# Windowed attention followed by a sine-gated MLP on one core: attention output written straight into the full x, first loads reordered, mask setup cut, and the global-token inserts moved from the MLP part to the attention part

## The chip, the cores and the metric

The kernel runs on one core of one Trainium2 chip. The metric is the time of one execution on the device in microseconds (us), as the median of several executions. Each kernel was also run once under the hardware profiler, and all readings of a profile below are from that execution. Its length is called the span; it is 2.2 us below the median for the kernel before.

Five engines work in parallel, and the text uses the profile's names for them: PE (matmuls; PEld is its weight load), DVE (vector engine), ACT (scalar engine, activation functions), POOL (GpSimd), and SP, which here only issues DMAs. DMAs are also issued by POOL and by ACT, and an issue takes time on the engine's queue.

## The reference, cut to what matters

```python
# q, k, v: (8 batches, 8 heads, 576 tokens, 64); 8 global token indices
def _attn_ref(q, k, v, global_idx):
    scores = (1 / sqrt(64)) * q @ k^T
    mask = |i - j| <= 32, or i is global, or j is global
    attn = softmax(where(mask, scores, -1e9))
    return attn @ v

def _moe_ref(x, w_in, w_out, alpha):       # x: (4608, 512); d_ff = 2048
    h = x @ w_in
    s = np.sin(alpha * h)
    g = h + s * s / (alpha + 1e-09)
    return g @ w_out
```

x is the attention output, with the heads side by side. All matmuls of the kernels run in bf16.

## The kernel before

The kernel walks through nine iterations p. Iteration p does attention of batch p (for p below 8) and then the first matmul of the MLP for chunk p of 512 tokens. The second matmul of chunk p-1 fills PE's gaps during attention of batch p. A batch has 576 tokens and a chunk 512, so eight batches give nine chunks, and the last iteration has no attention.

Attention is cut into 8 units: 4 head pairs (hp) times 2 halves (hf) of the tokens. A unit is scores `Sp` (PE), `E = exp` (ACT), `E * MASK` (DVE), the denominator `den` (PE), its reciprocal as exp(-ln) (ACT), the numerator `num` (PE), and numerator times reciprocal (DVE). These names are in the profile lines below.

The key tile `kTw` of a head pair holds, for each window of 48 queries, 112 window keys and then 8 global keys; `qBD` holds 48 queries and then 8 global queries. The transposes (`stage_T`) bring the batch's own keys and queries, and `globals_in` inserts the global ones, on POOL:

```python
    def globals_in(b, hp):
        nc.gpsimd.tensor_copy(out=kTw[hp][:, :, KB : KB + NG], in_=GT[:, 0, hp, b, ...])
        for t in range(2):
            nc.gpsimd.tensor_copy(out=qBD[hp][pr, :, t, QB:QC], in_=GT[pr, 1, hp, b, ...])
```

Attention writes into a tile of its own batch, `xTb`. At the end the rows of the global tokens are scattered into it by POOL, and DVE copies it to the chunk tiles `xC`, because a chunk spans two batches:

```python
    def stage_G(b, xTb, gn, gd):
        # ... gr = 1 / (gd[0] + gd[1]); gs = gn[0] + gn[1]; xg = gs * gr, on DVE
        for j in range(NG):
            nc.gpsimd.tensor_copy(out=xTb[:, :, bass.ds(pregs[j], 1)], in_=xg[:, :, j : j + 1])
        for c in range(...):                       # the chunks that this batch touches
            nc.vector.tensor_copy(out=xC[c][:, :, ...], in_=xTb[:, :, ...])
```

The first MLP matmul has 16 slots of 128 hidden units. Each slot does 4 matmuls, a sine on ACT, a square on DVE or POOL, and `H2b = S2 * recip + h` on DVE. In slot 10 the next batch's global inserts and the transposes of its first head pair are put in, in slot 13 those of the second:

```python
                eng = nc.vector if nt % 4 == 3 or (c == 0 and nt % 2) else nc.gpsimd
                eng.tensor_tensor(out=S2[:], in0=Sb[:], in1=Sb[:], op=ALU.mult)
    # ...
                def nxt(p=p, psB=psB):
                    shift_v(p + 1)
                    global_v(p + 1)                 # DMA: global values into VW
                    for hp in range(NHP):
                        globals_in(p + 1, hp)
                    stage_T(p + 1, 0, psB, "hb")
                m1.insert(10, nxt)
                m1.insert(13, partial(stage_T, p + 1, 1, psB, "hb"))
```

The prologue loads batch 0, builds the mask and gathers the global tokens' q, k and v. The mask has to know which windows already hold a global token as an ordinary key (`flag`). It gets there through POOL steps that take DVE's results:

```python
    # after the loads, and after about 20 memsets on DVE:
    nc.vector.memset(gcol[:].bitcast(DT.int32), 0)
    nc.scalar.dma_start(out=gcol[KB : KB + NG, :], in_=global_idx[:, None])
    # ...
    nc.vector.tensor_scalar(out=EQ[:], in0=Gf[:], scalar1=Gp[:, 0:1], op0=ALU.is_equal)
    nc.gpsimd.affine_select(out=EQ[:], in_=EQ[:], ...)                   # POOL waits for DVE
    nc.vector.tensor_reduce(out=flag[:], in_=EQ[:], op=ALU.max)          # DVE waits for POOL
    nc.vector.tensor_scalar(out=flag[:], in0=flag[:], ...)
    for base, cm in (...):
        nc.gpsimd.affine_select(out=flag[:], in_=flag[:], ...)           # and again
    # ... DQ = (distance > 32) * flag on DVE
    nc.vector.tensor_tensor(out=MASK[:, :, 0:QB], in0=MB[:], in1=DQ[:], op=ALU.max)
```

The softmax here doesn't subtract the row's maximum and nothing guards it: scores larger than these inputs give would overflow.

## Time and profile before

The time before was 444.24 us (median of three runs, 440.4 to 445.32). The profiled execution took 442.0 us. The page's first part gives busy time per engine, its share of the span, and the number of instructions:

```profile
PE 346.8 (78%) x2396; PEld 183.1 (41%) x2440; DVE 298.1 (67%) x628; ACT 269.3 (61%) x453; POOL 275.1 (62%) x447
```

No engine is full, so averages don't tell what bounds the kernel, and it has to be read stage by stage. Three points in time mark the stages, read from the timeline of PE: the first MLP matmul of an iteration ("MLP start"), the first den matmul of the next attention, and the next MLP start. This table holds them for the kernel before:

| Stage | us |
|---|---|
| start to first den of attention 0 | 36.1 |
| first den of attention 0 to MLP start 0 | 22.4 |
| MLP start 0 to MLP start 1 (period 1) | 53.0 |
| periods 2 to 7 | 44.7, 44.7, 44.6, 46.1, 44.5, 44.4 |
| of a steady period: MLP start to first den / first den to MLP start | 21.8 / 22.8 |
| last MLP start of an attention iteration to the end (tail) | 61.6 |

**The prologue.** The next lines are from the timeline of the kernel before, in order of start: start and duration in us, engine, line, operation, output<-input, count, and in brackets the idle time before it with what ended it.

```profile
16.26 0.32 ACTq L170 DMA_DIRECT2D gcol<-in_global_idx_dram  x1
25.48 0.13 DVE L193 CAST Gp<-gcol 128x1 f32<-128x1 int32 x1
...
28.88 0.18 POOL L201 TENSOR_SCALAR_AFFINE_SELECT EQ<-EQ 128x8 f32<-128x8 f32 x1
29.10 0.16 DVE L206 TENSOR_REDUCE flag<-EQ 128x1 f32<-128x8 f32 x1 [2.59 <-POOL EQ L201]
...
33.87 0.20 POOL L211 TENSOR_SCALAR_AFFINE_SELECT flag<-flag 128x1 f32<-128x1 f32 x1
34.10 0.52 DVE L245 TENSOR_SCALAR DQ<-DQ,flag 128x576 f32<-128x576 f32 x1 [3.36 <-POOL flag L211]
34.66 0.76 DVE L249 TENSOR_TENSOR MASK<-MB,DQ 128x576 bf16<-128x576 f32 x1
...
36.08 0.44 PE L352 MATMUL den<-E,ones_89 128*128 128x336 bf16 x1 [4.39 <-DVE E L342]
```

The scores were exponentiated by 30.92, but the den matmul ran at 36.08, because MASK was written only at 34.66 to 35.42. DVE twice waited for a POOL select of a fifth of a microsecond. On POOL these selects stood behind global inserts and weight-load issues. The index load itself was issued only at 16.26.

**A steady period.** Windows are busy times in a stretch; here the two halves of one steady period of the kernel before, MLP start to first den and first den to MLP start:

```profile
200.84:222.62 21.78, 17.30 (x102) 8.25 (x104) 16.31 (x25) 16.78 (x24) 18.11 (x28) 1.00 0.26 52
222.62:245.44 22.82, 21.24 (x181) 12.29 (x184) 16.32 (x48) 14.90 (x30) 13.32 (x24) 1.00 1.31 112
```

The columns after the length are PE, PEld, DVE, ACT and POOL busy, then the granted PE clock as a share of full speed, the time of the DMA packets as a share of 16 engines (above 1 where packets overlap) and GB/s. In the MLP half POOL is the busiest engine with 18.11 of 21.78 us, while in the attention half it has 9.5 us to spare. From the timeline, the end of POOL's chain and what hangs on it:

```profile
211.36 1.03 POOL L477 TENSOR_TENSOR S_2637<-Sb 128x512 bf16<-128x512 bf16 x1
...
212.34 0.26 POOL L285 COPY kTw_96<-GT 128x96 bf16<-128x96 bf16 x1
...
215.20 0.58 POOL L291 COPY qBD_103<-GT 64x96 bf16<-64x96 bf16 x2
215.87 1.04 POOL L477 TENSOR_TENSOR S_2678<-Sb 128x512 bf16<-128x512 bf16 x1
...
218.86 1.03 POOL L477 TENSOR_TENSOR S_2734<-Sb 128x512 bf16<-128x512 bf16 x1
...
221.41 0.74 DVE L455 SCALAR_TENSOR_TENSOR H2b<-S_2744,recipT,hb 128x512 bf16<-128x512 bf16 x1
222.07 0.91 DVE L342 TENSOR_TENSOR E<-E,MASK 128x672 bf16<-128x672 bf16 x2
...
222.62 0.30 PE L352 MATMUL den<-E,ones_89 128*128 128x336 bf16 x1 [1.87 <-DVE E L342]
```

From 212.34 to 215.78 POOL does inserts in the middle of its squares. Its last square ends at 219.89. DVE's H2b additions follow the squares, its multiplication by the mask follows the additions, and den follows that. The last stretch is DVE's own: once a POOL square has released it at 216.94, it runs without a gap to the mask multiplication, six additions and a square of its own (218.92, 1.25 us).

**The end of attention.** Three lines of the same timeline, from the last scatter to the next MLP start:

```profile
199.54 0.73 POOL L411 COPY xTb<-xg 128x4 bf16 x3
200.30 0.83 DVE L418 COPY xC<-xTb 128x1280 bf16<-128x1280 bf16 x2 [2.14 <-POOL xTb L411]
200.84 9.10 PE L465 MATMUL hb<-xC,w_in 128*128 128x512 bf16 x39 [0.75 <-DVE xC L418]
```

PE waits 0.75 us for the xC copy that follows the scatters.

### The profile page before, as it was taken

Reading aid. Unit: us, or ns where it says so; the run is one execution under the profiler, and the core shown is the slowest. Engines: PE = TensorE matmul, PEld = TensorE weight load, DVE = VectorE, ACT = ScalarE, POOL = GpSimd, SP = SyncE. Lnnn points to the kernel's source line nnn. Section 1 sums busy time; section 2 is a strip of 40 time slices with the busy share of each in tenths; the row PEclk is TensorE's granted clock in tenths of the full one; section 3 lists DMA queues with packets and bytes.
Section 4 is the critical chain, followed back from the end, with each engine's and each line's share of the span. In section 5 each row is a group of like instructions: output and inputs, shape, how many; then the busy total and the mean of one; then the engine's idle time right before and its main releaser. Section 6 shows DMA issues by size and latency. Waiting matters only on the chain.

```text
span 442.0 us, 7238 instructions
## 1 busy us (share of the span) xinstructions
PE 346.8 (78%) x2396; PEld 183.1 (41%) x2440; DVE 298.1 (67%) x628; ACT 269.3 (61%) x453; POOL 275.1 (62%) x447
## 2 busy tenths in 40 slices
PE   1036367599869997899789978998799879989996
PEld 0024223264436443554355445544454345434442
DVE  7556829767587758774878486848784878494520
ACT  0236636574778478756875686658775877564521
POOL 8956359881699269926992699249944910485410
PEclk9999969789999999999999998999999999999999
DMA  9939929996309830993099309940994000100111
GB/s 81 125 67 185 114 18 92 201 170 79 93 5 143 95 90 2 139 104 90 1 134 92 105 2 123 95 114 0 102 116 116 0 25 25 47 1 24 50 47 71
DMA packets 132055, 35.22 MB, mean 80 GB/s; under 512 B 123186, under 2 KB 126002, under 8 KB 132018
## 3 DMA queue, kind: packets, MB, share of 16 engines
q0 software_dynamic: 120896, 19.02, 58.8%
q1 hardware_dynamic: 8034, 15.54, 12.3%
q10 hardware_dynamic: 3088, 0.21, 0.6%
q8 instruction: 19, 0.31, 0.3%
q14 instruction: 18, 0.15, 0.1%
HBM read 38.42 MB, written 9.44 MB: 108 GB/s over the span
## 4 chain that ended last, share of the span: by engine, by line
POOL 33%; issue 27%; PE 16%; DVE 13%; DMA 5%; ACT 3%; POOLq 2%; ACTq 0%
DVE H2b L455 7%; PE ops L499 6%; PE hb L465 6%; DMA QS<-in_q_dram 4%; POOL QS L105 3%; POOL VW_104 L112 3%; POOL KS L105 3%; POOL VW_105 L112 3%; POOL xTb L411 3%; PE hb L499 2%; ACT L472 1%; POOL QS L100 1%; ACT Sb L472 1%; POOL KS L100 1%; POOLq L277 1%
## 5 line engine op out<-in xcount | busy, mean ns | idle before, releaser
L465 PE MATMUL hb<-xC,w_in 128*128 128x512 bf16 x559 | 134.1, 383 | 19.0 <-DVE xC L418 10.0
L472 ACT ACTIVATE Sb<-hb,alphaT 128x512 bf16<-128x512 f32 x144 | 94.5, 687 | 42.8 <-PE hb L465 35.8
L499 PE MATMUL ops<-w_out,H2b 128*128 128x512 bf16 x412 | 105.8, 384 | 2.0 <-ACT osb L506 0.7
L465 PEld LDWEIGHTS <-w_in 128*128 128x128 bf16 x576 | 56.3, 98 | 89.0 <-issue 28.7
L499 PEld LDWEIGHTS <-H2b 128*128 128x128 bf16 x576 | 53.9, 98 | 52.5 <-issue 2.3
L411 POOL COPY xTb<-xg 128x4 bf16 x64 | 12.9, 201 | 85.3 <-DVE xg L409 81.9
L384 DVE TENSOR_TENSOR xTb<-num,rec 64x288 bf16<-64x288 f32 x128 | 57.9, 452 | 7.9 <-PE num L375 6.8
L340 ACT ACTIVATE E<-Sp 128x672 bf16<-128x672 f32 x64 | 46.8, 731 | 14.8 <-PE Sp L333 14.3
L342 DVE TENSOR_TENSOR E<-E,MASK 128x672 bf16<-128x672 bf16 x64 | 31.8, 506 | 19.5 <-ACT E L340 18.5
L359 ACT ACTIVATE lnd<-den 128x288 f32<-128x288 f32 x64 | 26.2, 409 | 23.0 <-PE den L352 23.0
L105 POOL DMA_DIRECT2D QS<-in_q_dram x42 | 32.6, 775 | 6.0 <-DMA w_in<-in_moe_w_in_dram 3.3
L105 POOL DMA_DIRECT2D KS<-in_k_dram x42 | 33.0, 785 | 2.6 <-DMA w_in<-in_moe_w_in_dram 1.8
L506 ACT COPY osb<-ops 128x512 f32<-128x512 f32 x27 | 15.7, 581 | 30.0 <-PE ops L499 29.3
L352 PE MATMUL den<-E,ones_89 128*128 128x336 bf16 x64 | 20.3, 317 | 16.9 <-DVE E L342 16.4
L361 ACT ACTIVATE rec<-lnd 128x288 f32<-128x288 f32 x64 | 28.4, 443 | 2.0
L499 PE MATMUL qp<-w_out,H2b 128*128 128x512 bf16 x105 | 27.7, 379 | 0.4
L299 PE MATMUL Kps<-identb,KS 96*128 96x96 bf16 x192 | 14.7, 217 | 9.3 <-DVE Kps L152 6.4
L112 POOL DMA_DIRECT2D VW_105<-in_v_dram x28 | 21.4, 785 | 0.0
L333 PE MATMUL Sp<-qBD_100,kTw_96 128*128 128x112 bf16 x96 | 8.1, 227 | 16.9 <-DVE H2b L455 10.5
L375 PE MATMUL num<-E,VW_104 128*128 128x112 bf16 x192 | 15.0, 215 | 8.0 <-DVE gn L392 7.2
L112 POOL DMA_DIRECT2D VW_104<-in_v_dram x28 | 21.2, 768 | 0.0
L352 PE MATMUL den<-E,ones_90 128*128 128x336 bf16 x64 | 20.4, 319 | 0.0
(392 smaller groups left out, 605.6 us busy)
## 6 DMA issues: line engine op xcount, KB each, us to landing
out_dram<-osb SPq DMA_DIRECT2D x36, 256.0 KB
KS<-in_k_dram POOLq DMA_DIRECT2D x42, 96.0 KB, 4.0
QS<-in_q_dram POOLq DMA_DIRECT2D x42, 96.0 KB, 4.2
VW_104<-in_v_dram POOLq DMA_DIRECT2D x20, 112.0 KB, 5.1
VW_105<-in_v_dram POOLq DMA_DIRECT2D x20, 112.0 KB, 4.4
w_in<-in_moe_w_in_dram POOLq DMA_DIRECT2D x4, 512.0 KB, 7.9
w_out<-in_moe_w_out_dram POOLq DMA_DIRECT2D x4, 512.0 KB, 11.4
VW_104<-VW_104 SPq DMA_DIRECT2D x4, 384.0 KB
```

The source lines that it names most:

```text
L105: nc.gpsimd.dma_start(out=dst[:, t, :, :], in_=src[b, :, t * TW : (t + 1) * TW, :].rearrange("h p d -> p h d"),)
L112: nc.gpsimd.dma_start(out=W[p0 : p0 + n, par, u, :].rearrange("p (h d) -> p h d", d=D), in_=v[b, :, key0 : key0 + n, :].rearrange("h p d - ...
L340: nc.scalar.activation(out=E[:], in_=Sp[:, :, 0:EW], func=AF.Exp, scale=scale)
L342: nc.vector.tensor_tensor(out=Ev, in0=Ev, in1=MASK[:, hf * NU : (hf + 1) * NU, None, :].to_broadcast([P, NU, 2, QC]), op=ALU.mult,)
L352: nc.tensor.matmul(out=den[:].rearrange("p u c -> p (u c)"), lhsT=on[:], rhs=E[:].rearrange("p a (u t c) -> p (a u) t c", t=2, c=QC)[:, :, ...
L359: nc.scalar.activation(out=lnd[:], in_=den[:, :, 0:QB], func=AF.Ln)
L361: nc.scalar.activation(out=rec[:], in_=lnd[:], func=AF.Exp, scale=-1.0)
L384: nc.vector.tensor_tensor(out=xTb[pr, hp, hf * NU * QB : (hf + 1) * NU * QB].rearrange("p (a u c) -> p a u c", a=2, u=HU), in0=numv[pr, :, ...
L455: nc.vector.scalar_tensor_tensor(out=H2b[:, n_, :], in0=s_[:], scalar=recipT[:, n_ : n_ + 1], in1=h_, op0=ALU.mult, op1=ALU.add,)
L465: nc.tensor.matmul(out=h2[:], lhsT=w_in[:, ci, nt * P : (nt + 1) * P], rhs=xC[c][:, ci, :], start=(ci == 0), stop=(ci == CT - 1),)
L472: nc.scalar.activation(out=Sb[:], in_=h2[:], func=AF.Sin, scale=alphaT[:, nt : nt + 1])
L499: nc.tensor.matmul(out=ops[:], lhsT=H2b[:, nt, ts * P : (ts + 1) * P], rhs=w_out[:, nt, :], start=(nt == 0), stop=(nt == NT - 1),)
```

## The change

Its intent: attention writes its result straight into one tile `xT` of all tokens, which removes the copies to `xC`; the first loads are issued in the order of need; the mask is built from a band of three windows instead of twelve, with no POOL step that takes data from another engine; and the inserts for the next batch go from POOL's full MLP part to the attention part, where POOL has room. Part of the squares move too: in chunks 0 and 1 to ACT and DVE, later from every fourth on DVE to every fifth. Cut to its core:

```diff
+    xT = const.tile([P, CT, NTOK], BF, name="xT")
@@ setup: index loads and the zeroing of VW and Kps first, then the first four K/Q loads
-    nc.vector.tensor_scalar(out=EQ[:], in0=Gf[:], scalar1=Gp[:, 0:1], ...)
-    nc.gpsimd.affine_select(out=EQ[:], in_=EQ[:], ...)
+    # RF, a 0/1 tile made on POOL ahead of time, takes the place of the selects on data
+    nc.vector.scalar_tensor_tensor(
+        out=EQ[:], in0=Gf[:], scalar=Gp[:, 0:1], in1=RF[:, 1:], op0=ALU.is_equal, op1=ALU.mult)
@@
-    for base, cm in ((-KB, 1), (KB + NG - 1, -1)):
-        nc.gpsimd.affine_select(out=flag[:], in_=flag[:], ...)
+    nc.vector.tensor_tensor(out=flag[:], in0=flag[:], in1=RF[:, 0:1], op=ALU.mult)
-    MB = setup.tile([P, NW, QB], F32, name="MB")       # 12 windows
+    MB = setup.tile([P, 3, QB], F32, name="MB")        # first, inner, last window
@@ stage_V writes xT instead of xTb; stage_G:
-                out=xTb[:, :, bass.ds(pregs[j], 1)], in_=xg[:, :, j : j + 1]
-        for c in range(...):
-            nc.vector.tensor_copy(out=xC[c][...], in_=xTb[...])
+                out=xT[:, :, b * S : (b + 1) * S][:, :, bass.ds(pregs[j], 1)], in_=xg[...]
@@ mm1
-                        rhs=xC[c][:, ci, :],
+                        rhs=xT[:, ci, c * CH : (c + 1) * CH],
-                eng = nc.vector if nt % 4 == 3 or (c == 0 and nt % 2) else nc.gpsimd
+                eng = sq(nt)        # nc.scalar: activation(..., func=AF.Square)
+    sq_late = lambda nt: nc.vector if nt % 5 == 4 else nc.gpsimd
+    sq_early = lambda nt: nc.vector if nt % 2 else nc.scalar     # chunks 0 and 1
@@ attention of batch 0
+                    stage_T(0, 0, psA, "qp")
+                    globals_all()                      # cast, transpose, GT
+                    for hp in range(NHP):
+                        globals_in(0, hp, nc.vector)
+                    stage_T(0, 1, psA, "qp")
+                    globals_v_all()                    # VgN cast, recipT
+                    shift_v(0)
+                    global_v(0)                        # DMA VW<-VgN
+                    parts, last = attention(0, psA, {2: 7, 3: 11})   # head pairs 2, 3 at parts 7, 11
+                    with_extra(parts, w_loads, 6, 1)
+                    parts[6] = partial(chain, parts[6], pool_regs)
@@ attention of later batches: the next batch's inserts, on POOL
+                        for hp in range(NHP):
+                            i_ = (10, 12, 14, 16)[hp]
+                            parts[i_] = partial(chain, parts[i_], partial(globals_in, p + 1, hp))
@@ MLP part
-                    for hp in range(NHP):
-                        globals_in(p + 1, hp)
```

A part is one step of attention's unit loop, two for each unit and four ahead of them. Batch 1's loads, and part of batch 2's, move to the MLP part of the iteration before.

## The prediction

> **What bounds the kernel now.** No engine is full: the page has PE 78%, DVE 67%, ACT 61%, POOL 62% of 442.0 us. The timeline shows three stretches.
>
> 1. Prologue, 0 to 58.5 us, when the first MLP matmul starts. The first den matmul runs at 36.08, although the scores were exponentiated by 31. It waits for MASK: the gcol load is issued only at 16.26, behind memsets on DVE; then come POOL selects at 28.88 and 33.87, behind weight-load issues.
> 2. Steady periods, 44.6 us from MLP start to MLP start (e.g. 156.2, 200.84, 245.5). POOL works without pause from 204.01 to 219.88: 12 squares of 1.04 us and 3.3 us of global inserts. DVE's last H2b additions follow it, and attention's first den comes 21.8 us after MLP start (177.96 for the MLP from 156.2). POOL bounds the MLP part.
> 3. The end of attention: last num (195.8), xTb, gr, xg, eight POOL scatters (2.04 us), xC copies (0.83 us), MLP at 200.84. PE works off second matmuls until 200.1, so only 0.7 us is exposed.
>
> **What the change does.**
>
> - Mask: gcol is loaded at once, no POOL step waits for data, the band mask is a quarter in size. By order and durations, DVE finishes MASK near 19 us and the inserts near 22-23; ACT issues loads until 15.5, copies q, reloads its table (1.28). First den near 26 instead of 36. The rest of attention 0 took 22.4 us and loses 1.4 (xC, gr): MLP 0 starts near 47, 11.5 us earlier. Weights should land in time.
> - Batch 1: its loads move to MLP 0 (23 issues of 0.76 = 17.5 us on POOL), so ACT and DVE take the squares there. The inserts and two transposes precede attention 1 (about 4.5 us of latency), but PE does 24 second matmuls there. I expect about 49.5 us instead of 52.9: -3.
> - Period 2: ACT does 8 squares beside sine and copies, about 19.4 us: +1.
> - Periods 3 to 7: POOL has 13 squares instead of 12 plus inserts, and DVE's tail is shorter, as the last square is no longer its own (1.26 us beside POOL; 0.41 alone at 83.66). The Trainium skill, "SBUF — State Buffer", "Who interferes with whom", says that a DVE tensor_tensor with two SBUF inputs contends with GpSimd reads; those durations agree. First den about 18.6 us after MLP start instead of 21.8; 0.7 us from xC. About -3.3 to -3.9 each, -17 for five. The inserts fit between POOL's load issues (end 189.7) and its scatters (198.2).
> - Tail: +0.5 (13th POOL square).
>
> Sum: -11.5 - 3 + 1 - 17 + 0.5 = -30: **414 us, 80% range 402 to 426**. Chances: faster 0.95, same 0.04, slower 0.01.
>
> **What would show it.** First den near 26; first MLP matmul near 47; steady periods of 41 us; POOL's MLP stretch 2 us shorter; inserts in attention without delaying scatters; PE busy nearly unchanged (347 us).
>
> **What would make it wrong.** Weights or late heads arriving after need; PE falling to the halved clock (0.50 from 54 to 62 us after 5.3 us idle; the skill's "TensorE: Matmul & The Clock Gate", Part 1, has this) at attention 1's end, where no second matmuls remain; a second limit in the MLP part (ACT: sines, q copies and table loads are about 15 us) just below POOL; attention being PE-bound, so that an earlier start is lost later; POOL inserts blocking DVE's mask multiplications.

## The result, and the profile after

The changed kernel took 419.47 us (median of four runs, 418.45 to 419.92) against 444.5 us (440.4 to 445.32) of the kernel before, and is correct. The ratio is 0.945, with a 95% interval of 0.939 to 0.951. Here and below a ratio is the mean time of one kernel's fast runs over the mean of the other's fast runs of the same rounds, so it is not quite the ratio of the medians. A run counts as slow when it is over 1.5% above the fastest of its kernel. No run was (the kernel before spreads most, by 1.3%), so all count as fast. The profiled execution took 416.7 us. Busy time by engine:

```profile
PE 347.9 (83%) x2440; PEld 183.4 (44%) x2440; DVE 279.4 (67%) x636; ACT 277.1 (67%) x469; POOL 258.1 (62%) x418
```

PE's work is the same. DVE and POOL lost 19 and 17 us, ACT gained 8. Where the 25.3 us of the span went follows from the same marks as above:

| Stage | before | after | difference | predicted |
|---|---|---|---|---|
| start to first den | 36.1 | 25.5 | -10.6 | -10 |
| first den to MLP start 0 | 22.4 | 27.4 | +5.0 | -1.4 |
| period 1 | 53.0 | 48.9 | -4.1 | -3 |
| period 2 | 44.7 | 45.8 | +1.1 | +1 |
| periods 3 to 7, sum | 224.2 | 207.5 | -16.8 | -17 |
| tail | 61.6 | 61.6 | 0.0 | +0.5 |

One row has the wrong sign: attention 0 became longer. The timeline of PE of the changed kernel shows why:

```profile
25.49 0.72 PE L364 MATMUL den<-E,ones 128*128 128x336 bf16 x2 [1.37 <-DVE E L354]
...
30.64 0.74 PE L387 MATMUL num<-E,VW 128*128 128x112 bf16 x6 [2.97 <-DMA VW<-VgN]
...
33.30 0.68 PE L311 MATMUL Kps<-identb,KS 96*128 96x96 bf16 x6
33.78 0.68 PE L326 MATMUL qp<-identb,QS 96*128 96x96 bf16 x6
35.83 0.72 PE L345 MATMUL Sp<-qBD,kTw 128*128 128x112 bf16 x6 [1.37 <-ACT qBD L333]
```

Before that, the first den was held by something that the prediction doesn't have. The timeline of DVE of the changed kernel:

```profile
24.83 0.25 DVE L284 RECIPROCAL recipT<-alphaT 128x16 f32<-128x16 f32 x1 [1.63 <-DMA alphaT<-in_moe_alpha_dram]
25.00 0.86 DVE L354 TENSOR_TENSOR E<-E,MASK 128x672 bf16<-128x672 bf16 x2
```

E was exponentiated by 23.36, but DVE stood at a reciprocal of `alpha` for 1.63 us, waiting for the load of `alpha`, ahead of the multiplication by the mask. In run 6, whose edit doesn't touch this, the wait was 0.30 us and the first den came at 24.15. No run moved this load on purpose.

The first num waits 2.97 us for the DMA that puts the global values into VW. At 33.30 the head pair 2 is transposed, and the next matmul on PE is that head pair's scores, which wait for the copies of the transposes out of PSUM. The same happens with head pair 3 at 41.69, with a wait of 1.56 us for kTw. The DMA's issue is in the timeline of SP:

```profile
23.22 0.81 SPq L128 DMA_DIRECT2D VW<-VgN  x1
```

The steady period of the changed kernel, in windows from MLP start to first den and from there to MLP start:

```profile
188.79:208.37 19.58, 18.05 (x109) 8.72 (x108) 14.28 (x22) 16.93 (x25) 15.33 (x16) 1.00 0.22 53
208.37:230.38 22.01, 20.43 (x181) 11.98 (x181) 16.24 (x46) 14.66 (x30) 17.34 (x37) 1.00 1.42 120
```

POOL now has 15.33 us of work in the MLP half (18.11 before) and 17.34 us in the attention half (13.32 before), and both halves are shorter. The lines that end the MLP half, from the timeline of POOL, DVE, ACT and PE:

```profile
201.63 3.04 POOL L496 TENSOR_TENSOR S<-Sb 128x512 bf16<-128x512 bf16 x3 [0.28 <-ACT Sb L488]
...
205.18 2.72 DVE L471 SCALAR_TENSOR_TENSOR H2b<-S,recipT,hb 128x512 bf16<-128x512 bf16 x4
205.41 1.28 ACT L442 ACT_TABLE_LOAD   x1
205.47 1.04 POOL L496 TENSOR_TENSOR S<-Sb 128x512 bf16<-128x512 bf16 x1 [0.80 <-ACT Sb L488]
206.70 0.73 ACT L352 ACTIVATE E<-Sp 128x672 bf16<-128x672 f32 x1
207.82 0.50 DVE L354 TENSOR_TENSOR E<-E,MASK 128x672 bf16<-128x672 bf16 x1
208.37 0.45 PE L364 MATMUL den<-E,ones 128*128 128x336 bf16 x2 [0.43 <-DVE E L354]
```

POOL now waits for ACT's sines (0.28 and 0.80 us) instead of the other way round. ACT has E ready at 207.43, DVE finishes its additions at 207.90: two chains end half a microsecond apart. The end of attention has no copy any more; the MLP starts right behind the scatters:

```profile
188.01 0.73 POOL L425 COPY xT<-xg 128x4 bf16 x3
188.79 10.10 PE L481 MATMUL hb<-xT,w_in 128*128 128x512 bf16 x44
```

### The profile page after: what moved, and what is told of

Read it like the earlier page. It is cut to its first block, busy times and chain, and to the rows that moved or that the text cites. A ratio compares the mean times of both kernels' runs of the same rounds, so it can differ in the third digit from the quotient of the medians.

```text
span 416.7 us, 7242 instructions
## 1 busy us (share of the span) xinstructions
PE 347.9 (83%) x2440; PEld 183.4 (44%) x2440; DVE 279.4 (67%) x636; ACT 277.1 (67%) x469; POOL 258.1 (62%) x418
## 4 chain that ended last, share of the span: by engine, by line
PE 42%; ACT 18%; DVE 17%; issue 11%; POOL 10%; POOLq 1%; ACTq 0%
PE hb L481 15%; PE ops L518 13%; ACT Sb L488 7%; DVE H2b L471 6%; PE den L518 5%; DVE xT L397 5%; ACT qBD L333 4%; DVE E L354 3%; POOL S L496 3%; PE num L387 2%; ACT S L494 2%; PE den L364 2%; DVE gn L405 2%; PE hb L518 2%; ACT E L352 2%
## 5 line engine op out<-in xcount | busy, mean ns | idle before, releaser
L481 PE MATMUL hb<-xT,w_in 128*128 128x512 bf16 x576 | 137.5, 387 | 11.0 <-POOL xT L425 8.3
L471 DVE SCALAR_TENSOR_TENSOR H2b<-S,recipT,hb 128x512 bf16<-128x512 bf16 x144 | 101.3, 742 | 48.5 <-POOL S L496 48.5
L488 ACT ACTIVATE Sb<-hb,alphaT 128x512 bf16<-128x512 f32 x144 | 94.1, 685 | 39.6 <-PE hb L481 36.1
L496 POOL TENSOR_TENSOR S<-Sb 128x512 bf16<-128x512 bf16 x91 | 94.4, 1064 | 38.4 <-ACT Sb L488 33.6
L397 DVE TENSOR_TENSOR xT<-num,rec 64x288 bf16<-64x288 f32 x128 | 58.0, 453 | 8.7 <-PE num L387 6.8
L108 POOL DMA_DIRECT2D VW<-in_v_dram x56 | 42.4, 766 | 0.7 <-PE num L387 0.3
L345 PE MATMUL Sp<-qBD,kTw 128*128 128x112 bf16 x384 | 31.1, 220 | 14.0 <-ACT E L352 11.1
L387 PE MATMUL num<-E,VW 128*128 128x112 bf16 x384 | 30.4, 217 | 11.0 <-DVE gn L405 8.1
L333 ACT COPY qBD<-qp 64x576 bf16<-64x576 bf16 x40 | 25.1, 627 | 18.6 <-DMA gN<-in_v_dram 13.7
L525 ACT COPY osb<-ops 128x512 f32<-128x512 f32 x28 | 16.3, 582 | 27.8 <-PE ops L518 27.2
L364 PE MATMUL den<-E,ones 128*128 128x336 bf16 x128 | 30.1, 318 | 5.5 <-DVE E L354 3.9
L345 PEld LDWEIGHTS <-kTw 128*128 128x128 bf16 x384 | 24.5, 102 | 20.9 <-issue 13.9
```

The source lines that it names most:

```text
L108: nc.gpsimd.dma_start(out=W[p0 : p0 + n, par, u, :].rearrange("p (h d) -> p h d", d=D), in_=v[b, :, key0 : key0 + n, :].rearrange("h p d - ...
L333: nc.scalar.copy(out=qBD[hp][pr, :, t, 0:QB], in_=Qps[pr].rearrange("p (i c) -> p i c", c=QB),)
L345: nc.tensor.matmul(out=Sp[:, u // HU, o : o + 2 * QC], lhsT=kTw[hp][:, hf * NU + u, :], rhs=qBD[hp][:, hf * NU + u, :, :], start=True, sto ...
L387: nc.tensor.matmul(out=num[:, u // HU, o : o + 2 * QC], lhsT=W[:, i % 2, i // 2, hp * P : (hp + 1) * P], rhs=E[:, u // HU, o : o + 2 * QC] ...
L397: nc.vector.tensor_tensor(out=xT[pr, hp, x0 : x0 + NU * QB].rearrange("p (a u c) -> p a u c", a=2, u=HU), in0=numv[pr, :, :, t, 0:QB], in1 ...
L471: nc.vector.scalar_tensor_tensor(out=H2b[:, n_, :], in0=s_[:], scalar=recipT[:, n_ : n_ + 1], in1=h_, op0=ALU.mult, op1=ALU.add,)
```

## The experiments

Theories. For the steady periods the theory is the prediction's: POOL's chain of squares and inserts bounded the MLP half, and taking the inserts out of it is the main gain; the rivals are that the new division of squares or the missing xC copies made it. For the prologue the theory is that the mask (index load and POOL selects) was the last thing that attention 0 waited for in the kernel before, and that the changed kernel's loss afterwards comes from the late DMA of global values and from transposes standing directly before their scores. Twelve kernels ran, in four groups, each beside the kernel before on the same chip. "Before" below is the median of that group: 440.93 us (439.87 to 445.02), 442.01 us (439.9 to 444.75) and 444.06 us (439.77 to 445.08), and for run 12 443.76 us (439.99 to 444.9). The kernel before jumps by up to 1.3%, so medians of a few kernels are compared directly where a single microsecond counts: the changed kernels repeat within about 0.6%. The changed kernel itself was not run again in these groups, so a difference of about 1 us to its 419.47 us counts only where the traces show the stage that it comes from.

### 1. The inserts back in the MLP part (e1_inserts_back)

```diff
 # changed kernel
-                        for hp in range(NHP):
-                            i_ = (10, 12, 14, 16)[hp]
-                            parts[i_] = partial(chain, parts[i_], partial(globals_in, p + 1, hp))
@@ slot 10 of the MLP part
-    ... partial(global_v, p + 1), partial(stage_T, p + 1, 0, psB, "hb"))
+    ... partial(global_v, p + 1), *[partial(globals_in, p + 1, hp) for hp in range(NHP)],
+        partial(stage_T, p + 1, 0, psB, "hb"))
```

> The changed kernel with the global inserts of batch p+1 put back on POOL in MLP part p (p from 1), as before; squares, xT and prologue stay changed. Theory (POOL bounds the MLP part): POOL has 13 squares and 3.3 us of inserts, so the first den comes 21.5 to 23 us after MLP start instead of 19.6 and the steady period goes from 41.6 back to 44 to 45 us; whole kernel +14 to +20 us. Rival (the period shrank because of the removed xC copies and the shorter DVE tail, or ACT bounds the MLP part): period within 0.5 us of 41.6, whole kernel +0 to +3 us.

Measured: 433.53 us (432.67 to 434.73), ratio 0.980 (0.973 to 0.987). The steady period is 44.3 us (41.6 in the changed kernel); MLP start to den is 22.35 us (19.58), the attention half is 21.96 us (22.01). The window of one MLP half and the timeline of its end, for this kernel:

```profile
194.06:216.41 22.35, 19.41 (x109) 9.19 (x108) 14.67 (x22) 17.20 (x25) 18.68 (x28) 0.92 0.23 49
```

```profile
209.99 4.21 POOL L496 TENSOR_TENSOR S<-Sb 128x512 bf16<-128x512 bf16 x4
...
211.96 0.46 PE L345 MATMUL Sp<-qBD,kTw 128*128 128x112 bf16 x6 [2.19 <-DVE H2b L471]
...
213.23 2.71 DVE L471 SCALAR_TENSOR_TENSOR H2b<-S,recipT,hb 128x512 bf16<-128x512 bf16 x4
...
215.86 0.50 DVE L354 TENSOR_TENSOR E<-E,MASK 128x672 bf16<-128x672 bf16 x1
...
216.41 0.45 PE L364 MATMUL den<-E,ones 128*128 128x336 bf16 x2 [0.61 <-DVE E L354]
```

POOL is busy for 18.68 us of the half (15.33 in the changed kernel), its squares end at 214.20, the additions of DVE at 215.94 and the mask multiplication follows at once. So 14.1 of the 25 us of the whole change are undone by this one edit. In the traces, 14.6 of the 16.3 us by which the span grows lie in periods 3 to 7. The granted clock is 0.92 here, but den doesn't wait for PE: E was exponentiated by 213.79, and the mask multiplication waited for DVE's additions. The attention half cost nothing extra in the changed kernel, so the moved inserts are free there.

### 2. The old division of squares (e2_squares_old)

```diff
 # changed kernel
-    sq_late = lambda nt: nc.vector if nt % 5 == 4 else nc.gpsimd
+    sq_late = lambda nt: nc.vector if nt % 4 == 3 else nc.gpsimd
```

> The changed kernel with the old split of squares in MLP parts 2 to 8 (every fourth on DVE, so 12 on POOL and the last on DVE). Theory as predicted (the last square on DVE lengthens the tail by about 1 us): first den 20.5 us after MLP start instead of 19.6, period 42.5, kernel +4 to +6 us. Rival (with the inserts gone, ACT's sines, q copies and table load end last, and either split fits): first den and period within 0.4 us, kernel within 2 us.

Measured: 424.16 us (423.06 to 425.66), ratio 0.960. The steady period is 42.26 us (+0.7), with 20.27 us from MLP start to den. The last of the sixteen squares is DVE's own in this division. It takes 0.79 us there beside POOL's squares and stands before the last additions. The division is worth 4.7 us in the whole kernel, a third of the inserts.

### 3. The xC copies back (e3_xc_back)

```diff
 # changed kernel
-    xT = const.tile([P, CT, NTOK], BF, name="xT")
+    xbp, xcp: pools of xTb and xC as in the kernel before; stage_V writes xTb
@@ stage_G, after the scatters
+        for c in range(b * S // CH, ((b + 1) * S - 1) // CH + 1):
+            ...
+            nc.vector.tensor_copy(out=xC[c][:, :, ...], in_=xTb[:, :, ...])
@@ mm1
-                        rhs=xT[:, ci, c * CH : (c + 1) * CH],
+                        rhs=xC[c][:, ci, :],
```

> The changed kernel with attention writing a per-batch xTb and DVE copying it into chunk tiles xC, as before; all else changed. Theory (two copies of 0.83 us in all stand between the scatters and the first MLP matmul, but PE works off second matmuls until about the end of the scatters): den to MLP start 22.8 instead of 22.0 us, so +0.8 us per batch, kernel +5 to +7 us. Rival (the full x is what lets the next part start early, a large share of the gain): +2 us or more per batch, kernel +16 us or more.

Measured: 423.78 us (422.53 to 423.88), ratio 0.958. The attention half grows to 22.2 to 22.6 us, and the periods 4 to 7 by 0.2 to 0.4 us (41.75 to 42.03) rather than 0.8 (period 3 by 0.85); MLP start 0 comes 1.35 us later, where no second matmuls stand in between. The kernel is 4.3 us longer. So "writes straight into x" is worth about 4 us here, and in most steady periods about half of what the copy takes, or less.

### 4. In the kernel before, only the index load first (e4_before_gcol)

```diff
 # kernel before
+    setup = tc.alloc_tile_pool(name="setup", bufs=1)
+    gcol = ...; memset; nc.scalar.dma_start(out=gcol[KB : KB + NG, :], in_=global_idx[:, None])
     for i in range(2):
         nc.vector.memset(VW[i][0:32, 0, 0, :], 0.0)
     ...
-    (the same three lines, after the loads and memsets)
```

> The kernel before with only the small load of the global positions (and its memset) moved ahead of the DVE memsets. Theory (the late load holds MASK): EQ no longer waits, the scheduler puts the POOL selects ahead of inserts and weight issues, first den near 31 instead of 36.1, MLP 0 near 54 instead of 58.5, kernel -3 to -5 us. Rival (loads of K, Q, V hold attention 0, not the mask): MLP 0 at 58 to 59 and kernel within 1 us.

Measured: 445.5 us (442.41 to 446.18), ratio 1.007 (1.000 to 1.014), and the first den at 37.37, later than the 36.08 of the kernel before. The expectation missed. MASK itself was ready earlier, at 31.15 instead of 35.42, but the timeline of POOL and DVE shows what happened in its place:

```profile
27.39 0.19 POOL L201 TENSOR_SCALAR_AFFINE_SELECT EQ<-EQ 128x8 f32<-128x8 f32 x1 [3.01 <-issue]
27.62 0.16 DVE L206 TENSOR_REDUCE flag<-EQ 128x1 f32<-128x8 f32 x1 [6.59 <-POOL EQ L201]
```

With the index there early, the order of instructions on DVE changed: the reduction that needs POOL's select now stands ahead of the casts of the global tokens (28.31 here, 22.33 before). POOL came to its select only at 27.39, behind its register loads, and DVE idled 6.59 us. So the casts, their transposes, the inserts and the scores (first Sp at 33.22 instead of 29.44) were late instead of the mask. The wait moved; it was not removed. In this kernel the crossing between DVE and POOL holds den, not the load alone; run 5 shows what else stands behind it.

### 5. In the kernel before, the load first and the crossing removed (e8_before_flag)

```diff
 # e4_before_gcol, and in it
-    nc.gpsimd.affine_select(out=EQ[:], ...)         # on data
-    nc.gpsimd.affine_select(out=flag[:], ...) twice
+    RF = ...                                        # as in the changed kernel
+    nc.vector.scalar_tensor_tensor(out=EQ[:], in0=Gf[:], scalar=Gp[:, 0:1], in1=RF[:, 1:], ...)
+    nc.vector.tensor_tensor(out=flag[:], in0=flag[:], in1=RF[:, 0:1], op=ALU.mult)
```

> The kernel before with the early load of the positions and the row conditions built on POOL without data (as in the changed kernel), so that neither the mask nor DVE waits for POOL behind its register loads. Theory (both the late load and the in-order wait for POOL held attention 0): MASK ready near 25, inserts as in the kernel before at 28.5 to 29.7, first den near 31.7 instead of 36.1, MLP 0 near 54 instead of 58.5, kernel -3 to -5 us. Rival (the inserts behind POOL's register loads and the loads of weights bound attention 0 anyway): MLP 0 at 57 to 59, kernel within 1.5 us.

Measured: 442.34 us (441.5 to 443.09), ratio 1.001 (0.994 to 1.008): no difference that the rounds can show. The expectation missed. In the profiled execution the first den came at 33.67, 2.4 us earlier, and the span was 440.2 instead of 442.0 us. The timeline of this kernel:

```profile
26.70 0.74 DVE L253 TENSOR_TENSOR MASK<-MB,DQ 128x576 bf16<-128x576 f32 x1
...
27.91 0.26 POOL L289 COPY kTw<-GT 128x96 bf16<-128x96 bf16 x1 [2.17 <-DVE GT L273]
...
31.05 1.28 ACT L439 ACT_TABLE_LOAD   x1
...
32.34 0.73 ACT L344 ACTIVATE E<-Sp 128x672 bf16<-128x672 f32 x1
33.10 0.51 DVE L346 TENSOR_TENSOR E<-E,MASK 128x672 bf16<-128x672 bf16 x1 [2.98 <-ACT E L344]
```

The mask is ready at 27.44, 8 us earlier than before, and nothing waits for it. Den is now held by a second chain: global tokens, inserts, q copies on ACT, table load, exponential. In the kernel before, that chain had E ready at 30.92; here it has it at 33.07, 2.15 us later, because DVE now does its mask steps ahead of the work that this chain needs (the casts of the global tokens start at 24.06 instead of 22.33, the first copy of kTw at 27.70 instead of 24.72). So a faster mask could give the kernel before at most the 4.39 us that PE waited for it, and this run got 2.4 us of that. The changed kernel's first den is 10.6 us earlier, which needs the second chain moved as well, and the change moves it: the inserts of batch 0 run on DVE from 19.22, and the first exponential starts at 22.63 instead of 30.19. Which part of the change moved that chain was not tested apart.

### 6. Transposes earlier in attention 0 (e5_t_early)

```diff
 # changed kernel
-                    parts, last = attention(0, psA, {2: 7, 3: 11})
+                    parts, last = attention(0, psA, {2: 4, 3: 8})
```

> The changed kernel with the transposes of head pairs 2 and 3 of batch 0 at parts 4 and 8 of attention 0 (as in the other batches) instead of 7 and 11. Theory (placed directly ahead of the scores that need them, they expose their copies: PE stood 1.4 us at 35.8 and 1.6 us at 41.7): MLP 0 starts near 50 instead of 52.9, kernel -2.5 to -3.5 us. Rival (late heads: K and Q of heads 4 to 7 land too late for part 4, so that PE waits there instead): MLP 0 within 1 us of 52.9 or later.

Measured: 415.02 us (414.97 to 415.42), ratio 0.939: 4.45 us less than the changed kernel. MLP start 0 comes at 48.98 instead of 52.88. The first num still waits 2.88 us for the global values.

### 7. Global values earlier (e6_vgn_early)

```diff
 # changed kernel: the cast of VgN, shift_v(0) and global_v(0) go ahead of
 # the inserts and the second head pair's transposes; recipT goes after them
                     globals_all()
+                    globals_v_all()
+                    shift_v(0)
+                    global_v(0)
                     for hp in range(NHP):
                         globals_in(0, hp, nc.vector)
                     stage_T(0, 1, psA, "qp")
-                    globals_v_all()
-                    shift_v(0)
-                    global_v(0)
+                    nc.vector.reciprocal(out=recipT[:], in_=alphaT[:])
```

> The changed kernel with the cast of the global values, and so their insert into the value tile by DMA, ahead of the inserts of keys and queries for batch 0. Theory (the first num waited from 27.1 to 30.6 for that DMA, because it was issued only at 23.2 and then took 7.4 us): issued near 20, first num near 27 to 28, MLP 0 2.5 to 3.5 us earlier, kernel -2.5 to -3.5 us. Rival (the DMA engines are full of batch loads and weights until about 29, so an earlier issue lands no earlier): first num at 30 to 31, kernel within 1 us. Half of each: first num near 29.

Measured: 417.53 us (416.12 to 417.76), ratio 0.944: 1.9 us less. The DMA is issued at 19.74 instead of 23.22, but the first num starts at 28.33 instead of 30.64. So 3.5 us of an earlier issue gave 2.3 us of an earlier num, and 1.2 us at MLP start 0 (51.66). The semaphores in the traces date the landing: the transfer of 96 KB is in flight for 7.4 us in the changed kernel (landed 30.60) and for 8.5 us here (landed 28.29).

### 8. Both (e7_both)

> Both edits of the two runs before. Theory that they are two separate losses of the prologue: MLP 0 near 47, which is what the prediction had, kernel -5 to -7 us against the changed kernel. Rival (one hides the other, as the early transposes fill the wait for the global values): MLP 0 near 49 to 50, no better than the better of the two by over 1 us.

Measured: 413.97 us (413.56 to 414.95), ratio 0.937: 5.5 us less than the changed kernel. In its timelines of PE and PEld the first num stands right behind the second transposes, almost without a wait (its weight load waited 0.29 us for the DMA, which landed at 28.60):

```profile
27.40 0.69 PE L310 MATMUL Kps<-identb,KS 96*128 96x96 bf16 x6
27.88 0.68 PE L325 MATMUL qp<-identb,QS 96*128 96x96 bf16 x6
28.64 0.74 PE L386 MATMUL num<-E,VW 128*128 128x112 bf16 x6
...
28.64 0.50 PEld L386 LDWEIGHTS <-VW 128*128 128x128 bf16 x6 [0.29 <-DMA VW<-VgN]
```

MLP start 0 is at 47.78, with the first den at 25.23: 22.6 us for the rest of attention 0, as in the kernel before (22.4) and not 27.4 as in the changed kernel. Of the 6.4 us by which the changed kernel's attention 0 exceeds the predicted 21, these two edits take back 4.8 us; of the remaining 1.6 us, run 11 (21.8 us) gets another 0.8, and the rest is not explained. A rival is that PE's clock made the difference, because the groups of six score matmuls took 0.77 us up to 38 in the changed kernel and 0.46 us from 31 in this one. Run 2 speaks against it: with the prologue of the changed kernel untouched, its matmuls ran fast from 33.7 to 39.6 and slow from 41.15, and its MLP start 0 was 52.87, as in the changed kernel (52.88). The waits set the time there, not the matmuls.

### 9. DVE's squares early in the chunk (e9_squares_first)

```diff
 # e7_both
-    sq_late = lambda nt: nc.vector if nt % 5 == 4 else nc.gpsimd
+    sq_late = lambda nt: nc.vector if nt in (1, 5, 9) else nc.gpsimd
```

> Both prologue edits, and in MLP parts 2 to 8 the three squares of DVE at tiles 1, 5 and 9 instead of 4, 9 and 14 (POOL still has 13). Theory (with the inserts gone, the end of the MLP part is DVE's queue: it runs without a gap for the last 9 us and ends with four additions after its square of tile 14): a square taken early, while DVE waits for POOL, makes DVE free about 0.5 us earlier: first den 19.0 instead of 19.6, period 41.0, kernel -2 to -4 us against both prologue edits alone (413.97). Rival (ACT's sines and table load end last): no change of the period, within 0.2 us.

Measured: 412.4 us (412.23 to 412.71), ratio 0.931. The period is 41.39 us (41.59), MLP start to den 19.40 us. DVE's own late square at the end of the chunk, the theory, is worth about a third of what was expected (0.2 us of the period instead of 0.6). In the trace DVE's last two additions now each wait for a square of POOL (0.21 and 0.25 us) and end at 203.22, so POOL is the limit again; ACT had E ready at 202.95, 0.27 us before.

### 10. One more copy from ACT to DVE (e10_squares_q)

```diff
 # e9_squares_first: in the MLP part, one of the two q copies of head pair 0 goes to DVE
-            nc.scalar.copy(out=qBD[hp][pr, :, t, 0:QB], in_=...)
+            cp = nc.vector.tensor_copy if (t == 1 and qtag == "hb" and hp == 0) else nc.scalar.copy
+            cp(out=qBD[hp][pr, :, t, 0:QB], in_=...)
```

> The run before, and one of the four q copies in the MLP part (0.63 us) moved from ACT to DVE. Theory (ACT and DVE end the MLP part nearly together, so both must be relieved): first den about 18.4 to 18.7 us after MLP start, period 40.5, kernel -4 to -6 us against 413.97. Rival 1 (DVE alone ends last): slower than the run before by 0.3 to 0.6 us per period. Rival 2 (ACT alone): this run gains 0.6 us per period, the run before nothing.

Measured: 412.1 us (411.86 to 412.78), ratio 0.931. The expectation (a period of 40.5, 4 to 6 us in all) missed: the steady periods do not gain (41.54 us), since what ACT saves DVE pays. Period 2, where ACT also has eight squares, falls from 45.36 to 43.92 us. Half of that is ACT's: the MLP half falls from 22.59 to 21.85 us. The other 0.70 us lies in the attention half, where PE ran at half clock for 3.4 us in run 9 (121.5 to 124.9) and not in this one. So ACT held part of period 2, about 0.7 us of it.

### 11. Register loads before the weight loads (e11_regs_first)

```diff
 # e7_both: POOL's eight register loads go ahead of its first weight load
-                    with_extra(parts, w_loads, 6, 1)
                     parts[6] = partial(chain, parts[6], pool_regs)
+                    with_extra(parts, w_loads, 6, 1)
```

> Both prologue edits, and POOL's register loads (about 5.4 us) ahead of the first weight load, so that this load (1 MB read) is issued near 27 instead of 24.4. Question: what kept the insert of the global values, issued at 19.7, from landing before 28.2. Theory (the first weight load competes for the DMA engines): first num near 27 or earlier, kernel within -2 to +1 us of 413.97. Rival (the loads of K and Q of the last heads, issued until 21.6, fill the engines): first num at 28 to 29 again.

Measured: 412.67 us (412.12 to 413.42), ratio 0.932. The first weight load is issued at 27.71. The first num starts at 28.59, where PE has just finished transposes. The semaphores in the trace tell when the global values landed: at 28.54, 8.1 us after their issue at 20.44, although the first weight load came only 0.8 us before that. In run 9, with the first weight load at 24.41, they took 8.1 us too. So the weight loads are not what makes this DMA slow. A rival is the K and Q loads of the last heads, still landing until 29.1 here: in the kernel before, where these had landed by 16.5, the same DMA took 3.9 us. No run moved them, so this is not shown. MLP start 0 is at 47.25 and period 1 takes 48.99 us instead of 50.02, so the kernel is 1.3 us shorter all the same.

### 12. All together (e12_all)

```diff
 # e7_both + register loads first + squares at 1, 5, 9
 # + the q copy on DVE only in the MLP part of period 2 (batch 2)
+            cp = nc.vector.tensor_copy if (t == 1 and qtag == "hb" and hp == 0 and b == 2) \
+                else nc.scalar.copy
```

> A version meant to beat the changed kernel: both prologue edits, register loads ahead of the first weight load, DVE's three squares at tiles 1, 5 and 9, and one q copy on DVE in MLP part 1 only (where ACT has squares as well; in the run with it everywhere, period 2 was 43.92 instead of 45.4 us and the later ones gained nothing). If the parts add up as their stages did: MLP 0 at 47.3, periods 49.0, 44.2, 41.0 and four of 41.4, then a tail of 61.1 us: a span of 408 us, 410 us as timed, ratio to the kernel before about 0.925. Rival (the stages disturb each other, as a shift by 1 us moves where PE falls to the halved clock): 412 to 413, no better than its parts.

Measured in five rounds: 410.82 us (410.3 to 411.39) beside 443.76 us (439.99 to 444.9), ratio 0.9256 (0.9235 to 0.9277). MLP start 0 is at 47.34, periods 1 to 7 are 50.04, 44.17, 40.98, and 41.38 or 41.37 for the other four. This version beats both kernels, by 8.65 us the changed one.

## Why the prediction was right or wrong

The prediction was 414 us with a range of 402 to 426, and 419.47 us was measured. The class, faster by over 2%, was right.

- **POOL bounds the MLP half: right, and shown.** Putting the inserts back costs 2.7 us a period and 14.1 us in all. The predicted POOL stretch "2 us shorter" was 2.8 us of busy time (18.11 to 15.33).
- **Periods 3 to 7, -17: right** (-16.8), with some luck: 1.5 us come from the disturbed period of 46.1 us of the kernel before. The undisturbed periods fell by 2.9 to 3.5 us where 3.3 to 3.9 were predicted, and the MLP half took 19.58 us instead of 18.6. The parts don't add up singly: undoing inserts, squares and xC costs 2.7, 0.7 and 0.4 us a period, 3.8 together, while these periods fell by 2.9 to 3.5 us, leaving out the one of the kernel before that was disturbed. Several chains end close together, and taking one away exposes the next.
- **The second limit just below POOL, named as a danger, is there.** In the changed kernel E is ready 0.47 us before DVE's additions end, and POOL waits for ACT. Runs 9 and 10 gained 0.2 us and nothing in the steady period.
- **Batch 1, -3: nearly right** (-4.1), **tail, +0.5: none** (0.0).
- **Period 2, +1: the number is right** (+1.1), **the mechanism in part.** Its MLP half grew from 21.78 to 23.75 us. ACT's squares are one part: with one copy less on ACT it took 21.85 and 22.09 us (runs 10 and 12). The other goes with PE's clock, which stood at 0.50 behind MLP start 1 in all changed kernels: where it stayed so for 5.5 us or more, this half took 23.75 to 23.81 us (changed kernel, runs 7 and 11), where for 3.0 to 3.5 us, 22.56 to 22.81 us (runs 1, 2, 6, 8 and 9). No run set the clock alone, so its share of about 1 us is not shown as a cause.
- **First den near 26: right** (25.49). The mask alone was worth at most 4.4 of the 10.6 us, and run 5, which moved it alone, got 2.4. The rest needs the chain of inserts, scores and exponential to be earlier too. The prediction had given the inserts and the table load times of their own, so its sum held. That it fits so closely is partly luck: this chain was ready about 1.5 us before its sum, and the load of `alpha`, which the prediction doesn't have, took the time back (24.15 in run 6).
- **The step that failed** is "The rest of attention 0 took 22.4 us and loses 1.4 (xC, gr): MLP 0 starts near 47, 11.5 us earlier". The term was mis-sized: MLP 0 started at 52.88, only 5.6 us earlier. The stage took 27.4 us instead of 21. It took for granted that attention 0 runs in the same way from an earlier start. Two things did not move along with it: the DMA of the global values, 7.4 us in flight, on which the first num waited 2.97 us, and the transposes of head pairs 2 and 3, which the diff put directly before their scores (parts 7 and 11). Moving both (run 8) gives MLP start 0 at 47.78 and 413.97 us, the predicted time. The prediction named "late heads arriving after need" as a danger, but the heads' data was there; what was late was their place in the order.
- **PE's work unchanged: right** (346.8 to 347.9 us). The halved clock that the prediction named for the end of attention 1 came: PE idled 4.21 us before MLP start 1 at 101.77, and the clock reads 0.50 from 100.47 to 107.29, where it was 1.00 before the change. At the end of attention 0 it was halved in both kernels (53.08 to 63.32 before, 49.27 to 56.09 after).

The kernel before had one period of 46.1 us, in which PE ran at half clock from 268 to 271. It was not tested whether such periods make its spread between 440 and 445 us.

## What to carry to other kernels

When an engine fills one phase and idles in the next, moving its small work across the boundary pays as long as the work is ready there and nobody waits for it in the new place: here 2.7 of the 3.4 us of POOL inserts came back per period, because attention had room for them. When a change brings a start forward, list everything that the stage after it takes from elsewhere (DMAs that need several us in flight, 3.9 to 8.9 us for the same 96 KB here, transposes placed by part number) and ask of each whether it moves along; the ones that don't become the new waits. When two chains end close together, removing one of them shows little, or even moves the wait (run 4), and only both together show the gain.

## What the Trainium skill lacked or had wrong

- "SBUF — State Buffer", "Who interferes with whom" says that a DVE instruction with two SBUF inputs contends with a GpSimd instruction that reads SBUF. The traces agree: a DVE square took 0.41 to 0.43 us with no square of POOL beside it, and 0.45 to 1.28 us with one (up to 2.42 us in chunk 0 of the kernel before). The section gives no durations for such a pair, and this was a term of the estimate. In the kernel before, two DVE squares ended 0.28 us after the POOL square that ran beside them, wherever they began (209.24, taking 1.26 us; 205.75, taking 0.58 us).
- "TensorE: Matmul & The Clock Gate", Part 1, puts the halved clock after at least one idle window of about 3.4 us. The drops here don't come out of such a window: the clock fell at 53.08 as PE's idle of 5.26 us began (kernel before), at 49.27, 0.5 us into the 4.13 us (changed kernel), at 268.12 after no wait longer than 1.87 us (kernel before), and at 212.89 after one of 2.19 us (run 1). In the 3.4 us before these four drops PE was busy for 0.37, 0.28, 0.38 and 0.36 of the time, and a low busy share was enough. Part 1 also tells of a kernel whose clock oscillated because PE idled briefly but often; it gives no busy share at which this begins.
- At the start this page lacks nothing: its table has the halved clock as the default state, and up to about 30 to 39 us matmul groups took 0.72 to 0.77 us where they later took 0.46 us. But the views show a granted clock of 1.00 there, because the trace has no clock record before the first one: a rise to full clock at 39.43 us in the kernel before, 39.02 in the changed one, 33.81 in run 2 and 29.58 in run 8. Ahead of that record durations have to be read instead.
- "ScalarE: Activation LUTs", "What ACT_TABLE_LOAD costs", gives about 1283 ns for the load and 1380 ns more for a drain, 2.66 us for a switch. The load was 1.28 us here, but the whole switch was 1.31 us: the last sine ended at 205.39 and the first exponential began at 206.70 in the changed kernel.
- "DMA: Bandwidth & Descriptors", "Anatomy of one DMA — SWDGE (gpsimd) path", has a fit for one DMA, about 2.0 us plus its bytes over 436e3, which would give an estimate of 2.2 us for 96 KB. That fit is for DMAs from GpSimd; the DMA of the global values, issued by SP, took 7.4 us from issue to landing in the changed kernel (up to 8.9 us in run 8), 5.2 us in steady periods, and 3.9 us in the prologue of the kernel before. The page gives no duration for a transfer that shares the engines with others, and the term that failed hung in part on such a time.
